# Linear attention and a token-mixing MLP on one core: six stores cut into row halves, and the last output tile made in two halves next to each other

## The chip, the core and the metric

The kernel runs on one core of a Trainium2 chip. Five engines work side by side, each through its own queue of instructions: TensorE (PE, matrix products; its weight loads are shown apart, as PEld), VectorE (DVE), ScalarE (ACT), GpSimd (POOL) and SyncE (SP), which here only issues DMAs and waits. The metric is the device time of one execution in microseconds (us). Time before: a median of 99.69 us over 8 runs, which were 99.25, 99.34, 99.50, 99.57, 99.81, 99.88, 99.91 and 281.49.

## The reference

Four batches, 8 heads, 768 positions, head size 64. A decayed linear attention works on blocks of 64 positions; its output, with the heads put side by side, is mixed over the positions and goes through a product with `w_out`.

```
for b in range(nb):                                   # blocks of 64 positions
    intra = einsum('bhic,bhjc->bhij', qb, kb) * Dmask
    intra = einsum('bhij,bhjd->bhid', intra, vb)
    inter = einsum('bhid,bhde->bhie', qb * lam_pow, kv_state)
    out[:, :, sl] = intra + inter
    kv_state = lam_block * kv_state + einsum('bhsd,bhse->bhde', kb_dec, vb)
...
wq, wk = x @ w_q, x @ w_k                             # x: (4, 768, 512)
W_tok = scale * einsum('bsd,btd->bst', wq, wk)
mixed = einsum('bst,btd->bsd', W_tok, x)
return maximum(mixed, 0) @ w_out                      # (4, 768, 512), float32
```

## The kernel before

**Tiling.** The attention is done for pairs of heads: 4 batches by 4 pairs give 16 units, each over six chunks of 128 positions. The MLP is done for each batch. Its last step, `mix_o(b, t, o)`, makes rows `t*128` to `t*128+127` of batch `b`: four matmuls of 512 columns into bank `o` of PSUM (one pool tile of eight banks). Then `mixed_o(b, t, o, eng)` copies the bank into a buffer `osb` of 128 rows by 512 float32 (256 KB) on DVE (`v`) or ACT (`a`), and SP issues the store of that buffer. There are 24 such tiles, six to a batch, and `outp` holds 12 buffers: the 13th copy waits for the store of the first.

**Order.** The string `ORDER` is the whole program order, written by hand. `O.2.4@6` is `mix_o(2, 4, 6)`, and `eo.2.4@6:v` the copy and store that belong to it. `Oh.3.5.1@5` is `mix_o_half`: the right 256 of the 512 columns of tile 5 of batch 3, in four matmuls of 256 columns; `oh.3.5.1@5:a` is `mixed_o_half`, which copies a half into the tile's buffer. The second half of a tile that is copied also issues the tile's one store, of all 128 rows. Before the change the last two tiles, 3.4 and 3.5, are made in halves: 3.5's right half early, right after tile 3.0, then 3.2, 3.1, 3.3, both halves of 3.4, and 3.5's left half last.

**Queues and semaphores.** POOL issues all loads of q, k, v and the weights; they are in float32 and come into the buffers as bf16. SP issues in this order: the load of `lam`; a tiny copy `held` (line 543) that waits for the load of k of unit 14, so that nothing behind it starts early; then the 24 stores. The order in which stores are issued is that of `ORDER`. The built program gives SP's DMAs eight semaphores in turn, number 0 to 7 and again from 0. Each DMA is first held until the one before it on the same semaphore has landed, so at most eight are out at once. SP issues 26 DMAs, so tile 3.4's store has semaphore 0 and the last store, tile 3.5's, has semaphore 1.

**The end.** On leaving the tile context (line 595) SP runs nine wait instructions in a row. The first looks at two semaphores of POOL's loads. The next eight look at SP's DMA semaphores 0, 1, 2 to 7, in this order, each together with one of another queue. Then comes a drain on SP, and a barrier of all engines.

Of the kernel before, what the change touches and what calls it, by code (L numbers as in the profile page):

```python
# [15 lines left out]
CH = 128  # L16
# [6 lines left out]
R = (slice(0, 64), slice(64, 128))  # L23
# [38 lines left out]
em.2.0@4:v Q.3.1@7 eo.1.3@6:a Q.3.0@2 eQ.3.1@7:v O.2.4@6 eQ.3.0@2:a K.3@7 eo.2.4@6:v O.2.2@2  # L62
eK.3@7:a Y.3@3 eo.2.2@2:v O.2.5@7 YA.3@3:a YB.3@3:v YC.3@3:v m.3.0@4 eo.2.5@7:v m.3.3@2 m.3.1@0
em.3.0@4:a O.2.3@6 em.3.1@0:v em.3.3@2:a m.3.2@4 eo.2.3@6:v O.2.1@7 em.3.2@4:a O.2.0@6 eo.2.1@7:v
O.3.0@4 eo.2.0@6:a Oh.3.5.1@5 eo.3.0@4:v O.3.2@6 oh.3.5.1@5:a O.3.1@7 eo.3.2@6:a O.3.3@6
eo.3.1@7:v Oh.3.4.0@5 eo.3.3@6:v Oh.3.4.1@4 oh.3.4.0@5:a
Oh.3.5.0@7 oh.3.4.1@4:v oh.3.5.0@7:a
"""


# [1 line left out]
def kernel(  # L72
# [11 lines left out]
    nc = tc.nc  # L84
# [55 lines left out]
    def load_wo(_):  # L140
# [26 lines left out]
        out=ET[:, 0:CH], data0=step, data1=step, initial=-1.0, op0=ALU.add, op1=ALU.bypass  # L167
    )
    for at, n in ((CH, CH), (2 * CH, 2 * CH), (4 * CH, 2 * CH)):
        nc.vector.tensor_tensor(  # L170
            out=ET[:, at : at + n], in0=ET[:, 0:n],
# [5 lines left out]
        out=ident.rearrange("e (p r) -> e p r", r=2), in0=natural,  # L177
# [4 lines left out]
        out=mask1, in0=ET[:, 0:CH], in1=row.to_broadcast([128, CH]), op=ALU.is_ge  # L182
# [4 lines left out]
        out=back, in0=ET[:, 0:CH], in1=row.to_broadcast([128, CH]), op=ALU.is_equal  # L187
# [4 lines left out]
        out=E6, in0=ramp[:, CH - 1 : CH + S - 1 : CH], in1=row.to_broadcast([128, NCH]), op=ALU.add  # L192
# [30 lines left out]
    def copy(eng, to, of):  # L223
        return (nc.scalar.copy if eng == "a" else nc.vector.tensor_copy)(out=to, in_=of)  # L224
# [287 lines left out]
    def mixed_o(b, t, o, eng):  # L512
        osb = outp.tile([128, HD], F32, tag="osb", name="osb")
        copy(eng, osb, PS[:, o, :])
        nc.sync.dma_start(out=out[b, t * CH : (t + 1) * CH, :], in_=osb)


    def mix_o_half(b, t, half, o):
# [27 lines left out]
    def zeros(count, o):  # L546
# [13 lines left out]
        M0=masked(0), M1=masked(1), Mc=drawn, Mm=masked_late, P=states("halves"), Pw=states("whole"), G=summed, Gp=added, I=inter, V=values, ex=attended, F=flip,  # L560
        ef=flipped, eg=flipped_half, Q=mix_q, eQ=mixed_q, K=mix_k, eK=mixed_k, Kh=mix_k_half, ek2=mixed_k_half, Y=mix_y, YA=mixed_y, YB=crossed_y(0), YC=crossed_y(1), Qp=mix_q_part, m=mix_m,
        em=mixed_m, eh=mixed_m_half, O=mix_o, eo=mixed_o, Oh=mix_o_half, oh=mixed_o_half, Z=zeros,
    )
    for word in ORDER.split():
# [35 lines left out]
```

## Time and profile before

| what | value |
|---|---|
| median of 8 runs | 99.69 us |
| the profiled execution, whole | 99.88 us |
| its span in the profile | 97.7 us |
| granted TensorE clock | 0.95 of full speed |
| PE busy | 90.6 us, 93% |
| DVE, ACT, POOL busy | 75.9, 58.4, 64.5 us |
| output stores | 24 of 256 KB, median 2.2 us from issue to landing |

The span starts with the first recorded instruction and ends with the last, so that 2.2 us of the profiled execution lie outside it. "Landing" is the moment at which a DMA's semaphore has its full count. A row such as `89.13 0.45 PE ps L521 x4` in the chain of waits gives the start in us, the length, the engine, the tile written, and the line.

### The profile page before, as it was taken

To read this page: it belongs to the slowest core of one execution; us is meant where nothing else is said; L and a number is where in the kernel's file an instruction comes from. 1 tells how busy PE (TensorE), PEld (TensorE's weight loads), DVE (VectorE), ACT (ScalarE), POOL (GpSimd) and SP (SyncE) were. 2 spreads that over 40 slices of the span, in tenths; PEclk is the share of its full clock that TensorE was granted. 3 is DMA by queue.
4 is the path that set the end of the run, shared out by engine and by line. 5 is a ranking of instruction groups with operands and counts; after the bars stand their busy time and mean duration, and the time that the engine had idled before them with its cause. 6 is when DMAs were issued, how large, how long until landed. Compare 5 with 4: busy or idle time off the path is not lost.

```text
span 97.7 us, 3427 instructions
## 1 busy us (share of the span) xinstructions
PE 90.6 (93%) x1471; PEld 59.1 (60%) x1471; DVE 75.9 (78%) x140; ACT 58.4 (60%) x96; POOL 64.5 (66%) x67
## 2 busy tenths in 40 slices
PE   5999999989999889989999999999999999999930
PEld 3355677578577557867745656579698754335510
DVE  5526899999589999787796997978999985773420
ACT  5585142547484887657628864099899962553220
POOL 5999999599999999999996999983600000000000
PEclk9999999999999999999999999999999999999999
DMA  0999999999999999999999999999992013337582
GB/s 1 93 143 160 165 158 168 157 163 168 160 163 168 163 166 164 161 177 193 174 160 163 149 143 156 159 161 331 399 402 103 0 52 122 155 152 272 220 327 102
DMA packets 67438, 16.60 MB, mean 170 GB/s; under 512 B 63840, under 2 KB 64352, under 8 KB 67424
## 3 DMA queue, kind: packets, MB, share of 16 engines
q0 software_dynamic: 63792, 10.10, 139.9%
q1 hardware_dynamic: 3632, 6.30, 16.9%
q8 instruction: 11, 0.18, 0.7%
q14 instruction: 3, 0.02, 0.1%
HBM read 20.19 MB, written 6.29 MB: 271 GB/s over the span
## 4 chain that ended last, share of the span: by engine, by line
PE 75%; ACT 9%; DVE 9%; issue 2%; DVEq 0%
PE ps L504 20%; PE ps L549 11%; PE ps L378 6%; PE ps L241 6%; PE ps L267 6%; PE ps L250 5%; PE ps L400 4%; PE ps L311 4%; PE ps L355 4%; PE ps L475 3%; ACT pr L293 3%; DVE qT L256 2%; PE ps L343 2%; DVE pr L281 2%; PE ps L451 2%
## 5 line engine op out<-in xcount | busy, mean ns | idle before, releaser
L281 DVE TENSOR_TENSOR pr<-ps,mask 128x768 bf16<-128x768 f32 x24 | 22.4, 951 | 0.5 <-PE ps L267 0.5
L504 PE MATMUL ps<-wo,rmT 128*128 128x512 bf16 x88 | 22.3, 390 | 0.0
L229 POOL TENSOR_TENSOR fv<-fv,DvI 128x768 bf16<-128x768 bf16 x11 | 16.4, 1493 | 3.3 <-DMA fv<-in_v_dram 3.2
L118 POOL DMA_DIRECT2D fk<-in_k_dram x16 | 16.8, 1049 | 0.4 <-DMA fk<-in_k_dram 0.3
L122 POOL DMA_DIRECT2D fv<-in_v_dram x16 | 16.8, 1051 | 0.0
L114 POOL DMA_DIRECT2D fq<-in_q_dram x16 | 13.9, 870 | 1.5 <-POOLq L584 0.8
L224 DVE COPY osb<-ps 128x512 f32<-128x512 f32 (+1 forms) x14 | 9.4, 672 | 6.1 <-PE ps L504 5.7
L224 ACT COPY osb<-ps 128x512 f32<-128x512 f32 (+1 forms) x12 | 6.4, 534 | 11.8 <-PE ps L504 7.2
L504 PEld LDWEIGHTS <-rmT 128*128 128x128 bf16 x88 | 7.8, 99 | 8.7 <-issue 1.2
L549 PE MATMUL ps<-ramp 128*128 128x512 f32 (+3 forms) x22 | 11.1, 621 | 1.1 <-DVE ramp L162 1.1
L224 ACT COPY kT<-ps 128x768 bf16<-128x768 bf16 x12 | 9.4, 808 | 3.9 <-PE ps L250 3.5
L224 ACT CAST xnat<-ps 128x768 bf16<-128x768 f32 x11 | 8.8, 803 | 3.0 <-PE ps L355 2.8
L293 ACT CAST pr<-ps 128x768 bf16<-128x768 f32 x8 | 6.4, 802 | 6.6 <-PE ps L267 6.4
L256 DVE TENSOR_TENSOR qT<-ps,dq 128x768 bf16<-128x768 bf16 x16 | 8.8, 553 | 1.9 <-PE ps L241 1.6
L267 PE MATMUL ps<-qT,kT 64*128 64x128 bf16 x192 | 9.1, 218 | 0.2
L486 ACT ACTIVATE rmT<-ps 128x768 bf16<-128x768 f32 (+1 forms) x11 | 7.7, 726 | 1.8 <-PE ps L475 1.7
L311 PE MATMUL ps<-fv,fk 128*64 128x128 bf16 (+4 forms) x160 | 8.3, 234 | 0.2
L241 PE MATMUL ps<-ident,fq 128*64 128x128 bf16 x192 | 8.3, 226 | 0.1
L250 PE MATMUL ps<-ident,fk 128*64 128x128 bf16 x192 | 8.2, 221 | 0.0
L267 PEld LDWEIGHTS <-kT 64*128 64x128 bf16 x192 | 5.7, 94 | 4.0 <-DVE kT L224 1.5
L355 PE MATMUL ps<-fv,pr 128*128 128x64 bf16 x192 | 8.0, 194 | 0.0
L311 PEld LDWEIGHTS <-fk 128*64 128x64 bf16 x160 | 6.5, 110 | 2.0 <-issue 1.0
(68 smaller groups left out, 146.5 us busy)
## 6 DMA issues: line engine op xcount, KB each, us to landing
out_dram<-osb SPq DMA_DIRECT2D x24, 256.0 KB, 2.2
fq<-in_q_dram POOLq DMA_DIRECT2D x16, 192.0 KB, 6.7
fk<-in_k_dram POOLq DMA_DIRECT2D x16, 192.0 KB, 7.0
fv<-in_v_dram POOLq DMA_DIRECT2D x16, 192.0 KB, 7.2
wo<-in_moe_w_out_dram POOLq DMA_DIRECT2D x1, 512.0 KB, 8.7
wqk<-in_moe_w_q_dram POOLq DMA_DIRECT2D x1, 64.0 KB, 7.1
wqk<-in_moe_w_k_dram POOLq DMA_DIRECT2D x1, 64.0 KB, 6.8
lam_all<-in_lam_dram SPq DMA_DIRECT2D x1, 4.0 KB, 2.5
```

The source lines that it names most:

```text
L114: nc.gpsimd.dma_start(out=fq[n], in_=rows_q(n))
L118: nc.gpsimd.dma_start(out=fk[n], in_=rows(n, k))
L122: nc.gpsimd.dma_start(out=fv[n], in_=rows(n, v))
L224: return (nc.scalar.copy if eng == "a" else nc.vector.tensor_copy)(out=to, in_=of)
L229: (nc.gpsimd if eng == "p" else nc.vector).tensor_tensor(out=vn[n], in0=fv[n], in1=DvI[:, 2 * kk : 2 * kk + 2, :].unsqueeze(3).to_broadcas ...
L241: nc.tensor.transpose(to.rearrange("e (t r p) -> e r t p", t=2, r=2)[:, r], fq[n][:, hl, a, r * D : (r + 1) * D], ident,)
L250: nc.tensor.transpose(PSH[R[hl], o, c * CH : (c + 1) * CH], fk[n][:, hl, c, :], ident)
L267: mm(PS[:, o + hl, cc * CH : (cc + 1) * CH], kT[n][R[hl], c], qT[n][R[hl], c], start=True, stop=True, skip_group_check=True,)
L281: nc.vector.tensor_tensor(out=pr[n, a].rearrange("j l (c i) -> j l c i", c=3), in0=PS[:, o : o + 2, 0:HALF].rearrange("j l (c i) -> j l c ...
L311: mm(to[R[hl], c:end, :], fk[n][:, hl, c, :], vn[n][:, hl, c, :].unsqueeze(1).to_broadcast([128, end - c, D]), start=(c == 0), stop=(c == ...
L504: mm(PS[:, o, :], rmT[b][:, kt].rearrange("f n i -> f (n i)")[:, t * CH : (t + 1) * CH], wo[:, kt, :], start=(kt == 0), stop=(kt == 3),)
L549: mm(PS[:, o, 0:n], blank, blank[:, 0:1].to_broadcast([128, n]), start=True, stop=True)
```

## The change

Two edits. In `ORDER`, the right half of tile 3.5 is moved from behind tile 3.0 to the end; tile 3.4 is made whole, and copied whole by ACT; tile 3.5's right half goes to DVE and its left half to ACT, one after the other at the very end. In `mixed_o`, each tile of batch 0 is stored by two DMAs, of rows 0 to 63 and rows 64 to 127, instead of one of 128 rows. The columns of one row stay together (2 KB).

```diff
@@ ORDER
-O.3.0@4 eo.2.0@6:a Oh.3.5.1@5 eo.3.0@4:v O.3.2@6 oh.3.5.1@5:a O.3.1@7 eo.3.2@6:a O.3.3@6
-eo.3.1@7:v Oh.3.4.0@5 eo.3.3@6:v Oh.3.4.1@4 oh.3.4.0@5:a
-Oh.3.5.0@7 oh.3.4.1@4:v oh.3.5.0@7:a
+O.3.0@4 eo.2.0@6:a O.3.2@6 eo.3.0@4:v O.3.1@7 eo.3.2@6:a O.3.3@6
+eo.3.1@7:v O.3.4@5 eo.3.3@6:v Oh.3.5.1@4 eo.3.4@5:a Oh.3.5.0@7 oh.3.5.1@4:v oh.3.5.0@7:a
@@ mixed_o
-        nc.sync.dma_start(out=out[b, t * CH : (t + 1) * CH, :], in_=osb)
+        rows = R if b == 0 else (slice(0, CH),)
+        for r in rows:
+            nc.sync.dma_start(out=out[b, t * CH + r.start : t * CH + r.stop, :], in_=osb[r, :])
```

`R` is the pair of slices 0 to 63 and 64 to 127. In the built program SP then issues 32 DMAs (2, then 12 halves of batch 0 among 5 whole tiles of batch 1, then 13 whole tiles), so the last store has semaphore 7 and the one before it semaphore 6. The nine waits of the end keep their order. PE has eight rows fewer: four matmuls of 512 columns with four weight loads stand where eight of 256 columns with eight weight loads stood.

## The prediction
> **What bounds the kernel now.** I read the summary of engines first, then the end of the chain of waits, then SP's own rows behind it. PE is busy 93% of the span, so in the body only PE's work counts. The chain's last rows:
>
> ```profile
> 86.34 2.79 PE ps L504 x12
> 89.13 0.45 PE ps L521 x4
> 89.58 2.70 PE ps L504 x12
> 92.28 0.91 PE ps L521 x8
> 93.20 0.02 issue
> 93.22 0.43 DVE osb L224
> 93.65 0.01 issue
> 93.67 0.37 ACT osb L224
> ```
>
> The reader is to see that PE has no gap up to its end, and that compute is over at 94.04 (93.67 + 0.37) of a 97.7 us span. The last 3.7 us are a tail of stores and waits, in which no engine computes. The change works there.
>
> Next, the stores by narrow windows (start, landing). The first fence is the last store, tile 3.5's:
>
> ```profile
> L538 SPq DMA_DIRECT2D out_dram<-osb x1: 401/401/401, 94.1 to 94.1; - x1
> ...
> DMA to landing us min/median/max: 2.3/2.3/2.3
> ```
>
> The one before it, 3.4's, starts at 93.71 and lands in 2.1 us; 3.3's starts at 93.04 and lands in 2.0 us, as do all stores from 79.5 us up to there. So the last one is 0.3 us late. Why, is in the busy time by stretch (the last two numbers are DMA share and GB/s):
>
> ```profile
> 93.50:94.00 0.50, 0.13 (x2) 0.00 (x0) 0.14 (x1) 0.33 (x1) 0.00 (x0) 0.95 0.55 209
> 94.00:94.50 0.50, 0.00 (x0) 0.00 (x0) 0.00 (x0) 0.04 (x1) 0.00 (x0) 0.95 1.00 385
> 94.50:95.00 0.50, 0.00 (x0) 0.00 (x0) 0.00 (x0) 0.00 (x0) 0.00 (x0) 0.95 0.99 373
> 95.00:95.50 0.50, 0.00 (x0) 0.00 (x0) 0.00 (x0) 0.00 (x0) 0.00 (x0) 0.95 0.98 377
> 95.50:96.00 0.50, 0.00 (x0) 0.00 (x0) 0.00 (x0) 0.00 (x0) 0.00 (x0) 0.95 0.90 352
> 96.00:96.50 0.50, 0.00 (x0) 0.00 (x0) 0.00 (x0) 0.00 (x0) 0.00 (x0) 0.95 0.01 0
> ```
>
> The queues were half idle at 93.5 to 94, then full for 2 us: three stores came too close together. 262 KB at some 375 GB/s are 0.70 us each. A rule from these rows: a store lands at the later of its issue + 2.0 and the landing before it + 0.70. It gives 95.04, 95.74 and 96.44 for 3.3, 3.4 and 3.5; the rows give 95.0, 95.8 and 96.4.
>
> Then SP's waits at the end. In the window from 96.45 to 96.95:
>
> ```profile
> L595 SPq EVENT_SEMAPHORE  x7: 28/28/28, 96.5 to 96.8; - x7
> L595 SPq DRAIN  x1: 7/7/7, 96.9 to 96.9; - x1
> ```
>
> Seven waits and a drain. Narrower windows put the first at 96.48 to 96.49 and the last at 96.84 to 96.86, so they are (96.85 - 96.485) / 6 = 61 ns apart. Semaphore 0 (tile 3.4) was passed at 95.8. The first of the seven is semaphore 1, the last store; the other six are semaphores 2 to 7, whose stores had landed long before. They are passed for nothing, one after the other, with the whole core waiting: every other engine's own drain starts at 93.7 or before.
>
> **Part by part.**
>
> *Last semaphore.* With 32 DMAs the last store has semaphore 7. The waits for 0 to 6 then run while it is still in flight (semaphore 6, tile 3.4's, is a landing 0.7 us earlier), and only the drain follows it. Gain 6 x 0.061 = **0.37 us**. Bounds: 0 if something else were late, 0.37 at most.
>
> *Order of the last tiles, PE.* PE's columns are the same. A group of 4 x 512 takes 0.90 us (2.70 / 3), one of 4 x 256 0.455 us (0.91 / 2). From 89.13, where tile 3.0 ends, after the change: 3.2 to 90.03, 3.1 to 90.93, 3.3 to 91.83, 3.4 to 92.73, 3.5's halves to 93.19 and 93.64. Before, it ended at 93.20 + 0.45 = 93.65. So nothing is gained on PE; the four weight loads that go were beside matmuls. New waits of PE: tile 3.2 now starts 0.45 us sooner in bank 6, which ACT's copy of 2.0 empties at 88.27 + 0.59 = 88.86, 0.27 us before 89.13; tile 3.3 follows 3.2's copy (90.08 + 0.59 = 90.67) in the same bank, with 0.26 us to spare. Both are covered; if a cover failed, PE would lose the excess one for one.
>
> *Copies.* 3.4 goes to ACT whole, 92.77 to 93.36 (0.59, its 128x512 row). 3.5's right half is on DVE from 93.22 to 93.64, its left half on ACT from 93.67 to 94.04, as now. The profile says that the last ACT copy waits for DVE; PE's end at 93.65 is the same instant, and I take PE.
>
> *Stores of the tail.* Now 3.4's store is issued at 93.71, behind DVE's copy, and 3.5's cannot go before 94.1, when SP is done with it. Afterwards 3.3's goes at 92.59 (91.83 + 0.04 + 0.69 + 0.03), 3.4's at 93.39, 3.5's at 94.07: 0.8 and 0.68 us apart. By the rule they land at 94.59, 95.39 and max(96.07, 96.09) = 96.09. Gain 96.45 - 96.09 = **0.36 us**. Bounds: 0.06 (SP's issue alone) and 0.40 (a full 2.0 from 94.04). I take the rule's value, since it reproduces three landings.
>
> *Six more DMAs.* SP's burst, tiles of batches 0 and 1:
>
> ```profile
> 63.30 8.10 SPq L515 DMA_DIRECT2D out_dram<-osb  x11
> ...
> 79.49 9.72 SPq L515 DMA_DIRECT2D out_dram<-osb  x7
> ```
>
> 11 issues take 8.1 us, 0.74 each with the waits between. 17 at this price take 12.5 us and end at 75.8, against the next store at 79.49 and the first copy that needs an old buffer at 81.12, on DVE. So SP has 3.7 us to spare, and behind it nothing else is queued. The eight semaphores turn over sooner: the eighth DMA of the burst needs `held` to have landed (62.66 + 4.3 = 67.0), and the ninth the first half-store (63.3 + 5.0 = 68.3). These waits are long, but inside the 12.5 us by the same slack; the data of 2.9 MB at 400 GB/s takes 7.2 us in any case.
>
> No row shows a store of 64 rows. [...] The row nearest is the whole store at some 400 GB/s in this burst, by which the split costs nothing. [...] Its other effect is on the loads beside it:
>
> ```profile
> 68.52 1.47 POOL L229 TENSOR_TENSOR fv<-fv,DvI 128x768 bf16<-128x768 bf16 x1 [1.62 <-DMA fv<-in_v_dram]
> ```
>
> POOL waits for the last load of v until 68.52 and is done at 69.99; PE takes the result at 70.71. Slack 0.72 us, so a load that is sooner gains nothing and one that is up to 0.72 later costs nothing.
>
> **Sum.** 0.37 + 0.36 = 0.73 us. The profiled execution goes from 99.88 to 99.15 and its span from 97.7 to 97.0. It lies 0.19 above the median, so the median goes from 99.69 to **98.96**. What a measurement can tell from no change is about 0.3%, 0.30 us.
>
> **Rivals.**
> 1. *Only the waits go, 99.32.* The store is not sooner: 3.5 lands at 96.4 since something else, such as a slower turn on ACT, holds its issue. For it: the attribution of the last copy to DVE, which I read away. Against: the dip to 209 GB/s, which the new order fills. 12%.
> 2. *The last semaphore brings nothing, 99.33.* Only the store's 0.36 us stays, if the waits are not what the drain stands behind. Against: seven waits at equal steps and a drain directly after. 6%.
> 3. *Slower, 100.2.* Half-stores take the DMA engines' turns while v's last load is still coming. From the point where it lands over 0.72 us later, each us costs PE one; at 2.0 us later the result is 98.96 + 1.28 = 100.24. For it: 12 small DMAs [...] right at 63 to 68 us, where total traffic stays at 152 to 166 GB/s with DMA shares over 1. Against: before 67 us the stores hardly move anyway (total traffic rises to 377 GB/s only then), and at most eight halves are out at once, so fewer bytes compete than now. 9%.
> 4. *A bank turns late on PE, 99.2 to 99.6.* The 0.26 us covers fail in part. 6%.
> The forecast has the rest, 67%.
>
> **Range and chances.** The forecast's own range is 98.8 to 99.3: the bounds give 0.43 to 0.77 us of gain, taken from 99.69 at one end and at the other from 99.57, the median without the run of 281.49. Rivals 1, 2 and most of 4 take the upper end to 99.5; the lower is 98.5, where the fastest run (99.25) less 0.77 would be. Faster by over 0.3%: forecast, most of 1, 2: 0.79. Within: some of 1, 2 and 4: 0.12. Slower: rival 3: 0.09.
>
> **What would show it.** After the last landing only SP's drain, with no run of waits 61 ns apart: step one. Landings of 2.0 to 2.1 us for the last store with issue near 94.07, and no DMA dip before 94: step two. The next store after the burst still at 79.5, and PE without a new gap at 70.7, 89.1 and 90.9: covers held. The prediction is wrong if PE's end moves off 93.6, or if the last landing stays at 96.4.

## The result, and the profile after

The changed kernel takes 98.32 us (median of 20 runs, 97.96 to 99.47) against 99.71 us for the kernel before (57 runs). The ratio is 0.9882, with a 95% interval from 0.9862 to 0.9902: 1.2 us less. It leaves out the executions that are over 1.5% above the fastest of their kernel. The forecast was 98.96 us, 0.73 us less. The direction and the two mechanisms were right; the size was 0.45 us short by the ratio. The median lies below the forecast's own range of 98.8 to 99.3; the ratio, put on the 99.69 us from which the forecast started, gives 98.51, at the very edge of the full range of 98.5 to 99.5.

The profiled execution took 98.14 us, with a span of 96.3 us. The end of its chain of waits (start in us, length, what):

```profile
85.87 6.17 PE ps L503 x28
92.04 0.89 PE ps L522 x8
92.93 0.03 ACTq L223
92.95 0.04 issue
92.99 0.37 ACT osb L223
```

PE now runs seven whole tiles and then the two halves without a break. The last copy ends at 93.36. From there to the end of the span are 2.9 us, where there were 3.7.

The last store, from the windows on it:

```profile
L539 SPq DMA_DIRECT2D out_dram<-osb x1: 333/333/333, 93.4 to 93.4; - x1
...
DMA to landing us min/median/max: 2.0/2.0/2.0
```

It is issued 0.03 us after the copy, takes SP 0.33 us where it took 0.40, and lands 2.0 us later instead of 2.3. The busy time by stretch (last two numbers: DMA share, GB/s):

```profile
92.50:93.00 0.50, 0.41 (x4) 0.12 (x2) 0.42 (x1) 0.17 (x2) 0.00 (x0) 1.00 0.57 217
93.00:93.50 0.50, 0.00 (x0) 0.00 (x0) 0.00 (x0) 0.37 (x1) 0.00 (x0) 1.00 0.94 352
93.50:94.00 0.50, 0.00 (x0) 0.00 (x0) 0.00 (x0) 0.00 (x0) 0.00 (x0) 1.00 0.92 352
94.00:94.50 0.50, 0.00 (x0) 0.00 (x0) 0.00 (x0) 0.00 (x0) 0.00 (x0) 1.00 0.97 365
94.50:95.00 0.50, 0.00 (x0) 0.00 (x0) 0.00 (x0) 0.00 (x0) 0.00 (x0) 1.00 0.88 340
95.00:95.50 0.50, 0.00 (x0) 0.00 (x0) 0.00 (x0) 0.00 (x0) 0.00 (x0) 1.00 0.00 0
```

After 93.0 the queues are close to full and never over-full; the one half-idle stretch, 92.5 to 93.0, is the pause between stores 0.9 us apart, and no store is late for it (those of 3.4 and 3.5 land 2.0 us after issue). The data ends at about 95.0, some 1.7 us after the last copy; before, it ended at about 96.0, some 2.0 us after it.

SP's waits at the end, in the windows 93.5 to 94.9 and 94.9 to 95.6:

```profile
L596 SPq EVENT_SEMAPHORE  x8: 28/28/28, 93.8 to 94.8; - x8
...
L596 SPq DRAIN  x2: 7/7/7, 95.5 to 95.6; - x2
L596 SPq EVENT_SEMAPHORE  x1: 28/28/28, 95.4 to 95.4; - x1
```

Eight of the nine waits are over by 94.8, while the last store is in flight. Only the ninth, semaphore 7, is behind the landing, and the drain follows it at once.

### The profile page after: what moved, and what is told of

Read it like the earlier page. It is cut to its first block, busy times and chain, and to the rows that moved or that the text cites. A ratio compares the mean times of both kernels' runs of the same rounds, so it can differ in the third digit from the quotient of the medians.

```text
span 96.3 us, 3428 instructions
## 1 busy us (share of the span) xinstructions
PE 89.3 (93%) x1467; PEld 58.2 (60%) x1467; DVE 76.1 (79%) x140; ACT 58.0 (60%) x95; POOL 64.5 (67%) x67
## 4 chain that ended last, share of the span: by engine, by line
PE 68%; ACT 11%; DVE 8%; DMA 5%; issue 3%; POOL 1%; DVEq 0%; ACTq 0%; POOLq 0%
PE ps L503 21%; PE ps L266 6%; PE ps L377 6%; DMA fk<-in_k_dram 5%; PE ps L249 5%; PE ps L550 5%; PE ps L310 4%; PE ps L399 4%; PE ps L240 4%; PE ps L354 4%; PE ps L474 3%; DVE pr L280 3%; ACT kT L223 2%; ACT pr L292 2%; ACT xnat L223 2%
## 5 line engine op out<-in xcount | busy, mean ns | idle before, releaser
L249 PEld LDWEIGHTS <-fk 128*64 128x64 bf16 x192 | 6.0, 110 | 3.4 <-DMA fk<-in_k_dram 2.8
```

The lines of the kernel that those rows point to most:

```text
L249: nc.tensor.transpose(PSH[R[hl], o, c * CH : (c + 1) * CH], fk[n][:, hl, c, :], ident)
```

## The experiments

Twelve runs follow, of ten different kernels (the kernel before once more, the changed kernel twice, one other twice), on three chips, each beside executions of the kernel before on the same chip. The table comes first, since the text refers to it. In the expectations, T is the theory that the tail alone gains, S that the split gains in the body (all that lies before the tail), P that the new order gains on PE. "Tail" is the time from the end of the last copy to the end of the span in the profiled execution, read from the trace's records before rounding. "Outside" is a run's time less its span, over all runs of that kernel.

| kernel | median us | before, same chip | ratio (95% interval) | tail | outside |
|---|---|---|---|---|---|
| before (first profile) | 99.71 | | | 3.69 | 2.2 |
| changed (first result) | 98.32 | 99.71 | 0.9882 (0.9862 to 0.9902) | 2.98 | 1.76 to 1.88 |
| c0_before_again | 99.84 | 99.48 | 1.0034 (1.0009 to 1.0059) | 3.74 | 2.12 to 2.23 |
| e1_split_only | 98.81 | 99.48 | 0.9955 (0.9932 to 0.9978) | 3.34 | 1.76 to 1.88 |
| e2_order_only | 99.34 | 99.48 | 0.9981 (0.9956 to 1.0006) | 3.37 | 2.11 to 2.22 |
| e3_six_small_loads | 98.70 | 99.48 | 0.9945 (0.9923 to 0.9966) | 2.96 | 2.16 to 2.27 |
| f1_changed_again | 98.33 | 99.78 | 0.9851 (0.9801 to 0.9901) | 2.96 | 1.78 to 1.88 |
| f2_split_eight_tiles | 98.64 | 99.78 | 0.9912 (0.9873 to 0.9951) | 3.36 | 1.75 to 1.82 |
| f3_split_three_tiles | 98.37 | 99.78 | 0.9848 (0.9810 to 0.9886) | 3.13 | 1.77 to 1.83 |
| f4_quicker_tail | 98.52 | 99.78 | 0.9870 (0.9820 to 0.9919) | 2.95 | 1.74 to 1.83 |
| g1_changed_third | 98.64 | 99.59 | 0.9895 (0.9852 to 0.9939) | 2.95 | 1.76 to 1.84 |
| g2_small_loads_again | 98.88 | 99.59 | 0.9923 (0.9892 to 0.9955) | 2.96 | 2.16 to 2.27 |
| g3_stores_after_loads | 98.86 | 99.59 | 0.9898 (0.9846 to 0.9951) | 2.97 | 2.15 to 2.22 |
| g4_stores_earlier | 108.33 | 99.59 | 1.0868 (1.0814 to 1.0923) | 2.96 | 2.17 to 2.24 |

### The two parts, one at a time

The kernel before, once more, unchanged:

> The kernel before once more, unchanged, for the scatter and the granted clock beside its own runs. Theory T (tail alone: 0.37 us of waits, 0.36 us of store, and the rest of the measured gain is the TensorE clock of the profiled runs or the choice of runs): ratio 1.000 within 0.002, and runs whose granted clock is 1.0 about 0.4 us shorter than runs at 0.95. Rival S (the split itself gains in the body) and rival P (the new order gains on PE) expect the same ratio, and no such tie to the clock.

Measured 1.0034, with an interval that leaves out 1.000: the same kernel, loaded again on the same chip, differs from itself by 0.3%. So a ratio of one kernel carries some 0.3 us that its own interval does not show, and the tails have to carry the argument. The tie to the clock cannot be seen in the whole time: nearly all runs here were granted 0.99 to 1.00, and this kernel's profiled span at clock 1.0 is 97.7 us, the same as the first one's at 0.95. Inside the two profiles, two differences cancel. From the start of the last copy to YA (a step of batch 3's MLP, on ACT) to the end of PE's work are 10.41 us in the first profile and 10.11 in this one, 0.30 less; but the last load of v landed at 68.45 us in the first and at 68.85 in this one, 0.40 later.

The split alone:

```diff
-        nc.sync.dma_start(out=out[b, t * CH : (t + 1) * CH, :], in_=osb)
+        rows = R if b == 0 else (slice(0, CH),)
+        for r in rows:
+            nc.sync.dma_start(out=out[b, t * CH + r.start : t * CH + r.stop, :], in_=osb[r, :])
```

> The split of batch 0's stores alone, order of the last tiles as before; the last store has semaphore 7. T: -0.37 us (ratio 0.996): the six waits after the last landing go, the last store still lands 2.3 us after its issue. S: -0.8 us or more (0.992), with an earlier end of PE. P: -0.37 us.

The last store keeps its late landing, as every theory had it:

```profile
L540 SPq DMA_DIRECT2D out_dram<-osb x1: 399/399/399, 93.8 to 93.8; - x1
...
DMA to landing us min/median/max: 2.3/2.3/2.3
```

The tail is 3.34, 0.40 shorter than that of the control: the six waits. Ratio 0.9955, 0.45 us: nearer to T's 0.37 than to S's 0.8. PE's end, at 93.24 us, is 0.3 sooner than the control's 93.53, but not because of PE: from the last copy to YA on, both take 10.11 us.

The new order alone:

```diff
-O.3.0@4 eo.2.0@6:a Oh.3.5.1@5 eo.3.0@4:v O.3.2@6 oh.3.5.1@5:a O.3.1@7 eo.3.2@6:a O.3.3@6
-eo.3.1@7:v Oh.3.4.0@5 eo.3.3@6:v Oh.3.4.1@4 oh.3.4.0@5:a
-Oh.3.5.0@7 oh.3.4.1@4:v oh.3.5.0@7:a
+O.3.0@4 eo.2.0@6:a O.3.2@6 eo.3.0@4:v O.3.1@7 eo.3.2@6:a O.3.3@6
+eo.3.1@7:v O.3.4@5 eo.3.3@6:v Oh.3.5.1@4 eo.3.4@5:a Oh.3.5.0@7 oh.3.5.1@4:v oh.3.5.0@7:a
```

> The new order of the last tiles alone, whole stores; the last store has semaphore 1, so the six waits stay behind it. T: -0.36 us (0.996): the last store lands 2.0 us after its issue, and the issue is some 0.06 us sooner. P: -0.8 us (0.992), with PE's end sooner by 0.4 us at the same clock. S: -0.36 us.

Its store lands 2.1 us after issue, and the seven waits are back (window 96.1 to 96.8):

```profile
L594 SPq EVENT_SEMAPHORE  x7: 28/28/28, 96.3 to 96.6; - x7
L594 SPq DRAIN  x2: 7/7/7, 96.7 to 96.8; - x2
```

The tail is 3.37, 0.37 shorter than the control's. PE gained nothing, so rival P falls: from the start of the last copy to YA to the end of the last copy are 10.56 us here (83.61 to 94.17), against 10.51 in the control (83.43 to 93.94). The median moved by 0.14 us and the ratio's interval reaches 1.0006, so by its time alone this part is inconclusive.

The semaphore without the split:

```diff
     nc.sync.dma_start(out=lam_all, in_=lam.partition_broadcast(128))
+    for i in range(6):
+        spare = consts.tile([1, H], F32, name=f"spare{i}")
+        nc.sync.dma_start(out=spare, in_=lam.partition_broadcast(1))
```

> The new order, whole stores, and six small loads of one row right after that of lam, so that the last store has semaphore 7 without any split. T: -0.73 us (0.993), the same as the changed kernel within 0.2 us. S: -0.73 us, but 0.4 us slower than the changed kernel. P: -1.18 us, as the changed kernel.

In the window from 94.9 to 95.7 one wait is left:

```profile
L597 SPq DRAIN  x2: 7/7/7, 95.6 to 95.6; - x2
L597 SPq EVENT_SEMAPHORE  x1: 28/28/28, 95.5 to 95.5; - x1
```

The tail, 2.96, is the changed kernel's, with no half-store anywhere. The tail's gain therefore comes from the number of the last store's semaphore and from the order; the split is only one way to get to that number. By the ratio, 0.9945, the whole gain is 0.55 us, 0.6 less than the changed kernel's first one on another chip: so far that speaks for S, which expected 0.4.

### How many waits, and a quicker end

The changed kernel again:

> The changed kernel once more, beside another 60 or so runs of the kernel before on the same chip. T (the tail alone, 0.76 us as its trace shows, and the rest of the first ratio is scatter of the body between chips and builds): ratio 0.9925 within 0.0025, level with the kernel with six small loads (0.9945). S (the split gains in the body): 0.988 again.

0.9851, 1.5 us: more than the tail's 0.76 us once more, with an interval that leaves out T's 0.9925.

Eight tiles split, so that the last store is on semaphore 1 again:

```diff
-        rows = R if b == 0 else (slice(0, CH),)
+        rows = R if b == 0 or (b == 1 and t in (5, 3)) else (slice(0, CH),)
```

> The new order with eight tiles split instead of six, 34 DMAs of SP, so that the last store has semaphore 1 and the six waits are behind it again. T: ratio 0.996, 0.37 us slower than the changed kernel; from the end of the last copy to the end of the span 3.33 us as with the new order alone. S: 0.992 or less, since more is split. If splitting costs time in the body: over 0.998.

The waits are back (window 95.6 to 96.15):

```profile
L596 SPq EVENT_SEMAPHORE  x7: 28/28/28, 95.6 to 96.0; - x7
L596 SPq DRAIN  x2: 7/7/7, 96.1 to 96.1; - x2
```

The tail is 3.36, as expected: the same kernel loses 0.40 us of tail by two more DMAs early in the program. The ratio, 0.9912, is lower than T's 0.996 and agrees with S's figure; the waits alone do not explain the sum.

Three tiles split, last store on semaphore 4:

```diff
-        rows = R if b == 0 else (slice(0, CH),)
+        rows = R if b == 0 and t in (5, 3, 1) else (slice(0, CH),)
```

> The new order with three tiles split, 29 DMAs of SP, so that the last store has semaphore 4 and three waits are behind it. T: from the end of the last copy to the end of the span 2.94 + 3 x 0.061 = 3.12 us; ratio 0.994. If the waits cost nothing singly, but only a last wait that is not the last semaphore does: 3.33 us.

In the window from 95.3 to 95.72:

```profile
L596 SPq EVENT_SEMAPHORE  x4: 28/28/28, 95.4 to 95.6; - x4
L596 SPq DRAIN  x2: 7/7/7, 95.7 to 95.7; - x2
```

Semaphore 4 and three behind it. The tail of 3.13 lies between 2.96 (none behind) and 3.36 (six behind): 0.06 us for each wait. The time, 0.9848, does not show the lost 0.17 us; it is below the scatter that the control has.

A version meant to beat both:

```diff
-eo.3.1@7:v O.3.4@5 eo.3.3@6:v Oh.3.5.1@4 eo.3.4@5:a Oh.3.5.0@7 oh.3.5.1@4:v oh.3.5.0@7:a
+eo.3.1@7:v Oh.3.4.0@5 eo.3.3@6:v Oh.3.4.1@4 oh.3.4.0@5:a Oh.3.5.1@7 oh.3.4.1@4:v Oh.3.5.0@6
+oh.3.5.1@7:v oh.3.5.0@6:a
...
-        if whole:
+        if t == 5:
+            nc.sync.dma_start(out=out[b, t * CH : (t + 1) * CH, at], in_=part[b, t][:, at])
+        elif whole:
             nc.sync.dma_start(out=out[b, t * CH : (t + 1) * CH, :], in_=part[b, t])
...
-        rows = R if b == 0 else (slice(0, CH),)
+        rows = R if b == 0 and t != 4 else (slice(0, CH),)
```

> A version that may beat both: tile 3.4 is made in two halves that ACT and DVE copy side by side, so that its store is issued 0.17 us sooner, and the halves of tile 3.5 are stored one by one, 128 KB each; five tiles of batch 0 are split, so that the last store still has semaphore 7. T, with DMAs that move 0.35 us for each half: the last landing 0.17 us sooner than in the changed kernel, 2.77 us from the last copy to the end of the span. Rival: stores of 1 KB per row move more slowly, and the tail is level with the changed kernel's 2.94 us or longer.

Its last two stores, of 128 KB each:

```profile
L540 SPq DMA_DIRECT2D out_dram<-osb x2: 398/403/408, 94.1 to 94.5; - x2
DMA to landing us min/median/max: 1.9/2.0/2.1
```

Half the bytes still land 1.9 to 2.1 us after issue. DVE had two of the four copies in a row and was done with the second only at 94.0, so the first of the two stores went at 94.1; issuing it took SP 0.40 us, and the last store went at 94.5, 0.12 us after the last copy. The tail is 2.95, level with the changed kernel's 2.96. The rival's forecast of the tail came true: this way brought nothing more. That stores of 1 KB per row move more slowly was hardly to be seen: the last stretch with data, 95.5 to 96.0 us, has 330 GB/s, and the changed kernel's, 94.5 to 95.0, has 340.

### The rest of the gain: body or not

The tail explains 0.76 us of the 1.2 and 1.5 that the changed kernel had gained so far. S said that half-stores leave the last loads more of the DMA engines. Four kernels with the same tail ran on one chip:

> The changed kernel on one chip with the next three, which all have the same tail (new order, last store on semaphore 7, 2.96 us from the last copy to the end of the span). Scatter theory N (what goes beyond the tail's 0.76 us is scatter between chips and builds): level with the whole-store version with six small loads within 0.25 us. Body theory S (half-stores leave the last loads more of the DMA engines): 0.4 to 0.6 us faster than it.

> New order, whole stores, six small loads (as before in this study). N: level with the changed kernel within 0.25 us. S: 0.4 to 0.6 us slower.

The changed kernel has 98.64, the one with whole stores 98.88; by the runs' ratios 0.9895 and 0.9923. The difference is 0.24 us by the medians, 0.28 by the ratios, and 0.42 by the medians of those executions alone that the ratios use (98.46 and 98.88). That reaches from what N expected to what S expected, and the intervals overlap. The next two move the start of the stores:

```diff
 def hold(n):
-        nc.sync.dma_start(out=held, in_=fk[n][0:1, 0, 0, :])
+        nc.sync.dma_start(out=held, in_=fv[n][0:1, 0, 0, :])
...
-hold.14
+hold.15
```

> As the whole-store version with six small loads, but the copy that holds SP back waits for the scaled v of unit 15 instead of the load of k of unit 14: the first stores go at about 70 us, when all loads have landed. S: 0.4 us or more faster than with the earlier hold, level with the changed kernel, and no wait of PE or of POOL on a load at 64 to 69 us that is longer than its own. N: level with the earlier hold within 0.25 us.

```diff
-hold.14
+hold.12
```

> As the whole-store version with six small loads, but the copy that holds SP back waits for the load of k of unit 12: the first stores go some 2 us earlier, among the last loads. S: 0.5 us or more slower than with the later hold, with PE idle at 66 to 68 us for a load. N: within 0.25 us.

With no store before 70 us, g3 has 98.86 against g2's 98.88: no cost of whole stores to the loads shows at the present hold (six executions of g3, with an interval of 0.5 us to either side). Starting them earlier is another matter. SP's hold ended at 55.1 us against 63.8 in g2, 8.7 us earlier and not some 2 as expected, and then POOL and PE waited for loads (us in total, times, longest):

```profile
POOL fv L231 <- DMA fv<-in_v_dram: 10.5, 2, 5.4
...
PE ps L252 <- DMA fk<-in_k_dram: 4.7, 2, 3.9
PE ps L243 <- DMA fq<-in_q_dram: 2.9, 1, 2.9
```

The median is 9.5 us above g2's. So stores can get in the way of the loads, as S has it, but with the present hold no run shows that they do, or that the split helps there.

Where the excess is, the last column of the table says. In every run of each kernel with half-stores, time less span is 1.74 to 1.88 us; in every run of each kernel without, those of the kernel before among them, it is 2.11 to 2.27. The ranges do not touch. The spans of g1 and g2 themselves have the medians 96.7 and 96.65 over the same executions. So **the kernels with half-stores are 0.35 us shorter outside the recorded span**, neither in the body nor in the tail.

The records go on behind the span, and a difference shows there. These are g1 (with half-stores, span 96.57 us), and then g2 (without, 96.66 us):

```profile
97.70:98.20 0.50, 0.00 (x0) 0.00 (x0) 0.00 (x0) 0.00 (x0) 0.00 (x0) 0.50 0.04 16
98.20:98.70 0.50, 0.00 (x0) 0.00 (x0) 0.00 (x0) 0.00 (x0) 0.00 (x0) 0.55 0.00 0
```

```profile
97.70:98.20 0.50, 0.00 (x0) 0.00 (x0) 0.00 (x0) 0.00 (x0) 0.00 (x0) 0.50 0.00 0
98.20:98.70 0.50, 0.00 (x0) 0.00 (x0) 0.00 (x0) 0.00 (x0) 0.00 (x0) 0.50 0.06 16
```

By the trace's packet records, the 16 GB/s are one packet of 8 KB on a queue that the profile calls "instruction". It starts 1.62 to 1.66 us after the end of the span in the seven profiles without half-stores, 1.13 to 1.17 us in six of the seven with them, and 0.68 us in f4's.

Tail and outside together, against the control's tail of 3.74, make 0.75 us for e1 (measured 0.45), 0.73 for f2 (0.88), 0.96 for f3 (1.5), 1.13 for f1 (1.5) and 1.14 for g1 (1.05). What remains has both signs: the sum is too large for e1, e2 and e3 on the first chip and too small for all four kernels on the second. Kernels of one chip are measured against the same executions of the kernel before, whose spans have the median 97.3 us on the first chip and 97.6 on the second (15 executions), so much of what remains may be a shift of this common yardstick; that was not tested.

Inside the profiles, what differs in the body goes with the landing of the last load of v. Leaving out g4's, they have it at 68.03 to 69.19 us, with half-stores or without, and the last copy to YA starts 14.57 to 14.77 us later. The earliest and the latest, the changed kernel and f4:

```profile
68.10 1.48 POOL L228 TENSOR_TENSOR fv<-fv,DvI 128x768 bf16<-128x768 bf16 x1 [0.73 <-DMA fv<-in_v_dram]
...
82.80 0.37 ACT L223 CAST YA<-ps 128x256 bf16<-128x256 f32 x1 [1.27 <-PE ps L450]
```

```profile
69.26 1.47 POOL L229 TENSOR_TENSOR fv<-fv,DvI 128x768 bf16<-128x768 bf16 x1 [0.73 <-DMA fv<-in_v_dram]
...
83.86 0.37 ACT L224 CAST YA<-ps 128x256 bf16<-128x256 f32 x1 [1.27 <-PE ps L451]
```

POOL scales v as soon as it has landed (0.07 us later in both). In the built program the last three loads wait for earlier loads alone and not for PE, so it is not compute that holds them back. From the last copy to YA to PE's end, every profile at a clock near 1.0 then takes 10.11 or 10.12 us, with either order of the tiles. Earlier scatter does not carry through: the second copy to xnat on ACT starts at 16.2 us in e1 and at 17.2 in f2, and the last copy to YA at 83.14 and 82.95.

What makes the time outside the span shorter is open. In the built programs all kernels with half-stores have one thing more in common: DVE's queue has 192 instructions (194 in f4) where the others have 191, because a copy then waits for two stores and gets one wait instruction more. SP's queue does not sort them (68 to 73 with half-stores, 62 or 74 without), nor does PE's (2910 or 2918 in both groups). The packet behind the span goes with DVE's length too: 191, 192 and 194 instructions have it at about 1.6, 1.15 and 0.7 us, while three, six or eight split tiles (all at 192) have it at the same time. But f4, with the earliest packet, is no shorter outside the span than the others with half-stores, so it is not shown that the end of the execution waits for this packet. A kernel with whole stores and one idle instruction more on DVE would tell DVE's length from the half-stores; it was not tried.

## Why the prediction was right, and where it fell short

- *Last semaphore, 0.37 us.* Right. e1 has 0.40 of tail, f2 against f1 0.40, and f3 shows that it goes wait by wait.
- *Last store, 0.36 us.* Right. e2 has 0.37. The rule of "issue + 2.0 or 0.70 behind the landing before" held for the changed kernel: 0.7 us apart, both landing in 2.0.
- *The sum in the tail, 0.73 us.* Right: 3.69 to 2.98 in the first pair of profiles, 3.74 to 2.96 between the control and f1.
- *PE's end at 93.6.* The prediction named any other end of PE's work as a sign of being wrong, and the profile has 92.91 instead of 93.63. The order is not the cause. Of the 0.72 us, 0.42 lie before the last copy to YA, which the kernel before has here:

```profile
83.22 0.37 ACT L224 CAST YA<-ps 128x256 bf16<-128x256 f32 x1 [1.30 <-PE ps L451]
```

  The last load of v landed just as much earlier, at 68.03 instead of 68.45. The other 0.30 lie behind that copy, where the first profile took 10.41 us at a clock of 0.95, and the changed kernel and the control both 10.11 at 1.0. So the fall of the span between these two profiles, 1.4 us, is half the change's and half the two executions' own.
- *PE and the copies unchanged.* Nearly. At equal clock the new order costs PE nothing, and is 0.05 us longer from YA to the end of the last copy. The records show where: the last ACT copy starts 0.08 us after PE's end (92.91 to 92.99) where it took 0.04 before (93.63 to 93.67). In the built program that copy waits for four semaphores where its partner of before waited for two, which I had not priced; that this is the cause was not tried.
- *Six more DMAs, nothing.* Right in the sum. The rate of the nearest row, 400 GB/s for whole stores, does not hold for half-stores: they move about half of it. Busy time by stretch, the kernel before first:

```profile
70.00:71.00 1.00, 1.00 (x36) 0.83 (x36) 1.00 (x3) 0.81 (x3) 0.00 (x0) 0.95 1.05 397
71.00:72.00 1.00, 1.00 (x40) 0.91 (x38) 1.00 (x3) 1.00 (x3) 0.00 (x0) 0.95 1.07 408
```

```profile
70.00:71.00 1.00, 1.00 (x44) 0.93 (x38) 1.00 (x2) 0.99 (x2) 0.00 (x0) 1.00 0.92 211
71.00:72.00 1.00, 1.00 (x32) 0.82 (x28) 1.00 (x4) 1.00 (x3) 0.00 (x0) 1.00 0.87 203
```

  The DMA share is a little lower, about 0.9 for 1.06, and the bytes are half: 203 to 211 GB/s for 397 to 408, in a stretch in which the stores that SP issues are half-stores alone. Why the halves are slower was not traced. SP's burst took 12.6 us, as estimated (12.5), but began at 64.4 us instead of 63.3, since the load for which the hold waits came later, and so ended at 77.0 instead of 75.8. The cover held: the next store went at 79.18, with 2.2 us left of the 3.7.
- *A slack of 0.72 us behind the last load of v, so that an earlier landing gains nothing and one up to 0.72 us later costs nothing.* Not borne out. Over a range of 1.16 us of landings the last copy to YA follows to within 0.2 us. The sum took 0 from it and lost nothing by that, since the landing does not go with the change. For the same reason "in the body only PE's work counts" says too much: PE is busy, and the body still keeps time with the loads. How PE is held there was not traced.
- *Rival 3, slower through the last loads.* It did not come. A slowdown through the last loads shows in g4 alone, where SP's hold ended at 55.1 us and the median is 9.5 us above g2's.
- **The step that fell short** is in the sum: it took what lies around the span, 2.2 us, as given, and brought the median down by the span's gain alone. It became 1.81 us. With it the sum is 0.73 + 0.36 = 1.09 us, against 1.18 us by the ratio (1.18% of 99.7). The last 0.1 us is within the scatter that the control shows. Why the 0.36 us came is open, as said above.

## What to carry to other kernels

Look at what the program does after its last DMA has landed: waits that stand behind the slowest one are paid singly (0.06 us each here), so give the last transfer the last place in the list, by whatever changes the count. At the end of a store stream, lay the issue times as far apart as one transfer takes on the DMA engines (0.70 us here, estimated from 262 KB at some 375 GB/s); smaller stores did not help (f4's tail is 2.95 us, the changed kernel's 2.96). Before crediting a difference to the body, compare time less span across all runs: it sorted these kernels without one exception where medians could not. And before crediting a difference between two profiles to the change, see whether the last load landed at the same time in both, and at what clock each ran.

## What the runs showed of the hardware that was not expected

- The time outside the recorded span is not a constant of the chip: 1.74 to 1.88 us or 2.11 to 2.27 us, sorted by the program alone, on each of the three chips of the experiments. Behind the span, an 8 KB packet of an instruction queue comes at 0.7, 1.15 or 1.6 us, sorted by the program too.
- The body of these kernels keeps time with its last load, although PE is busy 93% of the span: 14.57 to 14.77 us from the landing to a fixed point in the last batch, over landings 1.16 us apart.
- Whole-tile stores started 8.7 us earlier among the casting loads (SP's hold ended at 55.1 us instead of 63.8 in g2) made the kernel 8.7% slower than before. With PE busy for 1.2 of the 8 us from 68 to 76, the granted clock also fell in the profile of g4, from 1.00 at 68 to 70 us to 0.50 at 72 to 78, where it stayed while PE took up work again:

```profile
72.00:74.00 2.00, 0.00 (x0) 0.00 (x0) 0.19 (x1) 0.00 (x0) 0.00 (x0) 0.50 1.26 317
...
76.00:78.00 2.00, 2.00 (x40) 1.81 (x36) 0.58 (x2) 0.80 (x1) 1.24 (x1) 0.50 0.03 2
```

- The same kernel loaded twice on one chip differed by 0.34%, with an interval that left out zero.
